# Fused attention and expert layers on one core: a product for four batches at once by way of device memory, and a fixed order from step 36

## The chip, the cores and the metric

The kernel runs on one core of one Trainium2 chip. The metric is the device time of one execution in microseconds, less is better. The engines are named as in the profile: PE (TensorE matmul) with its weight loads PEld, DVE (VectorE), ACT (ScalarE), POOL (GpSimd) and SP (SyncE, which issues the DMAs here).

## What is computed

```python
# q, k, v: 8 batches x 8 heads x 576 x 64;  phi: 8 x 8 x 576 x 32;  w1: 4 x 512 x 1024;  w2: 4 x 1024 x 512
a = softmax(phi, axis=2)                       # over the sequence
k_m = einsum('bhsm,bhsd->bhmd', a, k)          # 32 memory rows per head
v_m = einsum('bhsm,bhsd->bhmd', a, v)
attn = softmax(q @ k_m.T / 8)
x = (attn @ v_m), heads side by side           # 4608 x 512
p = domain_probs / domain_probs.sum(-1)
out = sum over 4 experts e of p[:, e] * (relu(x @ w1[e]) @ w2[e])
```

All values are float32.

## The kernel before

The kernel never forms x. For each batch and expert it multiplies v_m with w1 (the product `vw`, 256 rows of 8 heads × 32 memory rows, by 1024), and then attn with `vw`. Every operand of a large matmul is split into a rounded part (ACT's copy to float32r) and a rest (DVE's subtraction); a product of two such operands is three matmuls: high × high, high × low, low × high. So nearly every tile costs one piece on ACT and one on DVE, named below by its output: `w` (w1 and w2 splits, L118 and L119), `vw` (L379, L380), `kvs` and `tl` (k and v, L218, L219, L204, L205), `a` (softmax of phi, transposed, L187, L188), `AT` (attn transposed).

Batches go in four pairs (k = 0 to 3). A pair passes through 4 experts, each of 32 steps, which makes 128 steps for a pair and 512 in all (`PAIR`, `LAST`). A step s does:

- `first(s + 2)` (L405): six matmuls of attn and `vw` into a PSUM tile `p1`, 256 or 320 wide, then relu. ACT makes the high part of `h` (L427), DVE the rest (L429). At width 320 there is a second piece of 64, `hm`.
- `second(s)` (L434): h with w2, three matmuls of 512 for each of two tiles, or of three tiles where `hm` is complete, into `p2`. After 8 steps DVE adds the finished tiles into `acc` (L460, L462), and the last expert's go out.
- side work from a table `plan[s]`: the attention of the next two batches, and the splits and `vw` products of the next expert.

Side work of a batch: `phi_max`, `phi_exp`, `phi_norm`, `phi_turn` (softmax of phi, transposed); `kv_split`, `kv_mm` (k_m and v_m of four head pairs into PSUM tiles `x`); `kv_out` copies x to SBUF (`xs`, ACT L241), `kv_fold` transposes it (PE L249, into `kvp`), `kv_pick` takes the parts out (`kvT`); `write_vt` splits v_m into `vt`; then scores, softmax and `transposes`. `vw_mm` (L361) makes one product of v_m and w1 for a pair of batches, three matmuls (L364 to L366) into a tile `pv`, and `vw_out` (L369) takes it out in two halves of 64 rows, one for each batch.

The side tiles and `p1` share four PSUM buffers (tag `pm`). Loads go through a ring of `STAGE` tiles, all by SP, each issued some loads ahead (`stage_ahead`, L90). The prologue stands in `tc.manual_schedule()`, where each engine has its instructions in program order; from step 0 on a scheduler orders them.

Of the kernel before, what the change touches and what calls it, by code (L numbers as in the profile page):

```python
# [32 lines left out]
PSUM = bass.MemoryType.PSUM  # L34

# [13 lines left out]
STAGE = 5  # L49
KVS = 2  # L50
AHEAD = 2

# [3 lines left out]
VW_AT = 26  # L56

UNITS_EVEN = (0, 4, 6, 6, 7, 9, 10, 13, 16, 19, 22, 37, 42, 42, 46, 49, 49)
UNITS_EVEN_0 = (29, 33, 36, 37, 37, 39, 40, 43, 46, 49, 50, 64, 69, 73, 73, 80, 81)
UNITS_ODD = (63, 66, 68, 69, 69, 71, 72, 75, 78, 81, 84, 99, 104, 104, 109, 111, 112)  # L60
# [9 lines left out]
def body(ctx: ExitStack, tc: tile.TileContext, qm, qt, kv, kvt, phi, prob, w1, w2, out):  # L70
    nc = tc.nc
    pool = lambda name, **k: ctx.enter_context(tc.tile_pool(name=name, bufs=1, **k))
    const, wp, work, att = pool("const"), pool("wp"), pool("work"), pool("att")
    psum = pool("psum", space=PSUM)

    ident = const.tile([P, P], F32, name="ident")
    make_identity(nc, ident)
    kvT = [const.tile([P, 2, NP, 2 * M], F32, name=f"kvT{i}") for i in range(2)]
    for t in kvT:
        nc.gpsimd.memset(t, 0.0)  # L80
# [3 lines left out]
    def source(key):  # L84
        kind, *i = key
        return {"kv": kv, "kvt": kvt, "qm": qm, "qt": qt, "w1": w1, "w2": w2}[kind][tuple(i)]
# [45 lines left out]
    def unit_w2(k, e, j2, eng=nc.vector):  # L132
        def emit(raw):
            for i in range(2):
                t = wp.tile([P, 2, DM], F32R, name="w2", tag="w2", bufs=NJ + 2)
                split(t, raw[:, i, :], eng)
                w2t[k, e, 2 * j2 + i] = t
        return ("w2", e, j2), emit

# [36 lines left out]
    def phi_turn(b, g):  # L176
        if g == 0:
            st["a", b] = att.tile([P, NP, NC, 2, 2 * M], F32R, name="a", tag="a")
        ph, a = st["ph", b], st["a", b]
        tp = psum.tile([P, 4, 2, 2 * M], F32, name="tpa", tag="pm", bufs=4)  # L180
        for c in range(4):
            nc.tensor.transpose(
                tp[:, c].rearrange("p a m -> p (a m)"), ph[:, g, c * P:(c + 1) * P], ident
            )
        src = tp.rearrange("p c a m -> p a c m")
        dst = a[:, 2 * g:2 * g + 2, :4]
        nc.scalar.copy(dst[:, :, :, 0, :], src)  # L187
        nc.vector.tensor_sub(dst[:, :, :, 1, :], src, dst[:, :, :, 0, :].bitcast(F32))  # L188

    def phi_turn_tail(b):  # L190
        ph, a = st["ph", b], st["a", b]
        tp = psum.tile([P, NP, 2 * M], F32, name="tpb", tag="pm", bufs=4)
        for g in range(2):
            nc.tensor.transpose(
                tp[:, 2 * g:2 * g + 2].rearrange("p a m -> p (a m)"), ph[:, g, 512:], ident
            )
        nc.scalar.copy(a[:, :, 4, 0, :], tp)
# [24 lines left out]
    def kv_mm(b, hp, c2):  # L222
        if hp % 2 == 0 and c2 == 0:
            st["x", b, hp // 2] = psum.tile([P, 2, 2 * P], F32, name="x", tag="pm", bufs=4)
        x, a, t = st["x", b, hp // 2], st["a", b], st["kvs", b, hp, c2]
        for i in range(2):
            c = 2 * c2 + i
            lhs = a[:, hp, c].rearrange("p s m -> p (s m)")
            for s in range(2):
                nc.tensor.matmul(x[:, hp % 2, :], lhs, t[:, s, i, :], start=c + s == 0, stop=False)  # L230

    def kv_mm_tail(b, hp):
        nc.tensor.matmul(
            st["x", b, hp // 2][:, hp % 2, :],
# [4 lines left out]
    def kv_out(b, hp):  # L239
        xs = att.tile([P, 2 * P], F32, name="xs", tag="xs", bufs=2)  # L240
        nc.scalar.copy(xs, st["x", b, hp // 2][:, hp % 2, :])  # L241
# [11 lines left out]
    def kv_pick(b, g):  # L253
        kvd = kvT[b % 2][:, :, 2 * g:2 * g + 2]
        kvp = st["kvp", b, g].rearrange("p h w c -> p w h c")
        for i in range(2):
            r, m = slice(64 * i, 64 * i + 64), slice(M * i, M * i + M)
            if i == 0:
                nc.scalar.copy(kvd[r, :, :, m], kvp[r, :, :, m])
            else:  # L260
                nc.vector.tensor_copy(kvd[r, :, :, m], kvp[r, :, :, m])
        for i in range(2):
            r, m = slice(64 * i, 64 * i + 64), slice(M * i, M * i + M)
            lo = slice(2 * M + M * i, 2 * M + M * i + M)
            nc.vector.tensor_add(kvd[r, :, :, m], kvd[r, :, :, m], kvp[r, :, :, lo])
# [15 lines left out]
    def write_vt(b, a=slice(0, 2)):  # L281
        k, odd = b // 2, b % 2
        if ("vt", k) not in st:
            st["vt", k] = att.tile([P, NP, 2, P], F32R, name="vt", tag="vt", bufs=2)
        vt = st["vt", k].rearrange("p (a two) h c -> p a two h c", two=2)
        v = kvT[odd].rearrange("p w (a two) c -> p w a two c", two=2)
        for par in range(2):
            dst = vt[:, a, par ^ odd, :, 64 * par:64 * par + 64]
            src = v[:, 1, a, par, :]
            nc.scalar.copy(dst[:, :, 0, :], src)  # L290
            nc.vector.tensor_sub(dst[:, :, 1, :], src, dst[:, :, 0, :].bitcast(F32))
# [4 lines left out]
    def scores_mm(b, t0, q, hps=range(NP)):  # L296
        nt, n = tiles(t0)
        kvd = kvT[b % 2]
# [3 lines left out]
        for hp in hps:  # L302
            for i in range(nt):
                nc.tensor.matmul(  # L304
                    sc[:n, i, hp, :], q[:, hp, i * P:i * P + n], kvd[:, 0, hp, :],
# [3 lines left out]
    def scores_exp(b, t0):  # L309
# [7 lines left out]
        nc.vector.tensor_sub(av, scv, mx[:n, :nt * H].broadcast_to([n, nt * H, M]))  # L317
        nc.scalar.activation(av, av, AF.Exp, scale=float(D) ** -0.5)
        st["at", b, t0] = at
# [14 lines left out]
    def unit_scores(b, t0):  # L334
        def emit(q):
            scores_mm(b, t0, q)
            scores_exp(b, t0)
            soft(b, t0)
        return q_key(b, t0), emit

    def transposes(b, t0):
# [3 lines left out]
        at, at_t = st["at", b, t0], st["AT", b]  # L345
        tp = psum.tile([P, 2, 256], F32, name="tp", tag="pm", bufs=4)
        for i in range(nt):
            for g in range(2):
# [4 lines left out]
                )  # L353
        c = slice(t0 * P, t0 * P + nt * n)
# [6 lines left out]
    def vw_mm(k, fh, hp, tag):  # L361
        vt, w = st["vt", k], w1t[fh, hp]
# [6 lines left out]
    def vw_out(ps, fh, hp, odds):  # L369
        g = hp // 2  # L370
        for odd in odds:
            if hp % 2 == 0:
                vw[odd, fh, g] = att.tile(
                    [P, 2, 512], F32R, name="vw", tag=f"vw{odd}", bufs=4 + odd
                )
            q = (hp % 2) ^ odd
            r = slice(64 * q, 64 * q + 64)
            t = vw[odd, fh, g]
# [3 lines left out]
    def vw_out_by_copy(ps, fh, hp):  # L382
        g, r = hp // 2, slice(64 * (hp % 2), 64 * (hp % 2) + 64)
        if hp % 2 == 0:
            vw[0, fh, g] = att.tile([P, 2, 512], F32R, name="vw", tag="vw0", bufs=4)
        t = vw[0, fh, g]
# [5 lines left out]
    def vw_unit(k, e, fh, hp, odds, tag):  # L392
        vw_out(vw_mm(k, fh, hp, tag), fh, hp, odds)


    hs, mid, acc, po = {}, {}, {}, {}
# [8 lines left out]
    def first(s):  # L405
# [7 lines left out]
        for g in range(2):  # L413
            w = vw[odd, j // 4, g]
# [19 lines left out]
    def second(s):  # L434
# [13 lines left out]
        if j < NJ - 1:  # L448
            return
        if e == 0:  # L450
# [5 lines left out]
        for t, _ in left:  # L456
# [15 lines left out]
    def att_units(b):  # L472
        u = [lambda g=g: phi_turn(b, g) for g in range(2)] + [lambda: phi_turn_tail(b), unit_tail(b)]
        u += [unit_kv(b, hp) for hp in range(NP)]
        u += [lambda: write_vt(b)]
        u += [unit_scores(b, t0) for t0 in (0, 2, 4)]
        u += [lambda t0=t0: transposes(b, t0) for t0 in (0, 2, 4)]
# [5 lines left out]
    rest = [unit_scores(0, t0) for t0 in (2, 4)] + [lambda t0=t0: transposes(0, t0) for t0 in (2, 4)]  # L483
# [3 lines left out]
    for s, u in zip(REST_0, rest):  # L487
        at(s, u)

# [3 lines left out]
    for fh in range(2):  # L493
        for g in range(2):
            at(W1_1[2 * fh + g], unit_w1(0, 0, fh, g))
            for i in range(2):
                vw_at(VW_1[4 * fh + 2 * g + i], 0, 0, fh, 2 * g + i, (1,))
    for k in range(NG):
        for e in range(E):
            s = k * PAIR + e * STEPS  # L500
            nk, ne = (k, e + 1) if e + 1 < E else (k + 1, 0)
            if nk < NG:
                for j2 in range(4):
                    at(s + W2_AT[j2], unit_w2(nk, ne, j2))
                n = 0
                for fh in range(2):
                    for g in range(2):
                        at(s + W1_AT[2 * fh + g], unit_w1(nk, ne, fh, g))
                        for i in range(2):
                            vw_at(s + VW_AT + n, nk, ne, fh, 2 * g + i, (0, 1))  # L510
                            n += 1
        if k + 1 < NG:
            b = 2 * k + 2
            for bb, U in ((b, UNITS_EVEN_0 if k == 0 else UNITS_EVEN), (b + 1, UNITS_ODD)):
                s0 = k * PAIR
                at(s0 + U[0], lambda bb=bb: load_phi(bb))
# [34 lines left out]
    with tc.manual_schedule():  # L551
        raw = {key: take(later) for later, key in enumerate(early)}
        stage_ahead(len(early) + 4)
        nc.sync.dma_start(pt, prob)
        keep_warm(10)
        dve, gps = nc.vector, nc.gpsimd
        write_vt(1)
# [26 lines left out]
        for hp in (2, 3):  # L584
# [3 lines left out]
            if hp == 2:  # L588
                for i in range(2):
                    kv_fold(0, i)  # L590
        kv_pick(0, 0)
        write_vt(0, slice(0, 1))
        w1g = [raw["w1", 0, 0, g] for g in range(2)]
        for hp in (2, 3):
            kv_out(0, hp)
        split_w1(w1g[0], 0, 0, gps)
        q = raw["qm", 0, 0]
        scores_mm(0, 0, q, (0, 1))
        for hp in (2, 3):
            kv_fold(0, hp)  # L600
        kv_pick(0, 1)
        scores_mm(0, 0, q, (2, 3))
        split_w1(w1g[0], 0, 1, dve)
        write_vt(0, slice(1, 2))
        split_w1(w1g[1], 0, 2, gps)
        split_w1(w1g[1], 0, 3, gps)
        for i in range(2):
            t = wp.tile([P, 2, DM], F32R, name="w2", tag="w2", bufs=NJ + 2)
            nc.scalar.copy(t[:, 0, :], raw["w2", 0, 0][:, i, :])
            w2t[0, 0, i] = t  # L610
        scores_exp(0, 0)
        for i in range(2):
            t = w2t[0, 0, i]
            dve.tensor_sub(t[:, 1, :], raw["w2", 0, 0][:, i, :], t[:, 0, :].bitcast(F32))
# [5 lines left out]
        vw_out(pv[1], 0, 1, (0,))  # L620
        transposes(0, 0)
        keep_warm(4)
        vw_out(pv[3], 0, 3, (0,))
# [4 lines left out]
    for s in range(LAST):  # L628
        run_plan(s)
        first(s + AHEAD)  # L630
        second(s)
# [36 lines left out]
```

## Time and profile before

| | us |
|---|---|
| median of 3 runs (lowest, highest) | 1428.31 (1426.05, 1429.47) |
| the profiled execution | 1428.84 |
| its span, first to last instruction | 1427.1 |
| mean granted clock of PE | 0.996 of full |
| PE busy / DVE busy / ACT busy | 1412.3 / 837.2 / 620.2 |
| DMA | 115.20 MB, mean 81 GB/s |

In the rows of the profile, a group has its line, engine, operation, output<-input, shape, count, then busy time and mean ns of one, then the engine's idle time ahead of it and what ended that. A row of windows has start:end, length, then for PE, PEld, DVE, ACT and POOL the busy time and the number of instructions, then PE's granted clock, the share of DMA and GB/s. A row of the timeline has start, length, engine, line, and in brackets a wait ahead of it and its releaser; a row of the chain has start, length, engine, tile and line; a row of waits has the total, the number of times and the longest. A DMA row has KB each and the median us from issue to landing.

### The profile page before, as it was taken

What the parts mean: (1) busy time and instruction counts of PE and PEld (TensorE: products, weight loads), DVE (VectorE), ACT (ScalarE), POOL (GpSimd) and SP (SyncE); (2) the same over time, 40 slices, a digit from 0 to 9 for tenths busy, and PEclk for the clock granted to TensorE, in tenths of its full rate; (3) what the DMA queues carried; (4) which work ended last, traced back from release to release, by engine and by line L of the source; (5) the groups of instructions that cost most, each with busy time, mean ns of one, the idle gap of its engine ahead of it and who ended that gap; (6) DMA issues with size and microseconds to landing.
All of it is one profiled execution on the core that took longest, in us unless ns stands there. A gap on an engine that the chain in (4) does not pass through costs nothing.

```text
span 1427.1 us, 20830 instructions
## 1 busy us (share of the span) xinstructions
PE 1412.3 (99%) x7808; PEld 1233.5 (86%) x7808; DVE 837.2 (59%) x1853; ACT 620.2 (43%) x1543; POOL 27.8 (2%) x27
## 2 busy tenths in 40 slices
PE   7999999999999999999999999999999999999998
PEld 6888888888888888888888888888888888888887
DVE  7876638666385654837547375573846446272722
ACT  6655426453263533635335362452625234161521
POOL 3300000000000000000000000000000000000000
PEclk8999999999999999999999999999999999999999
DMA  6632303323141120412214121140323103030001
GB/s 245 198 118 75 121 28 126 104 64 104 39 161 61 64 89 16 137 58 78 94 63 135 59 88 65 46 130 18 107 75 96 60 25 94 1 119 1 1 30 38
DMA packets 35957, 115.20 MB, mean 81 GB/s; under 512 B 3984, under 2 KB 5136, under 8 KB 35856
## 3 DMA queue, kind: packets, MB, share of 16 engines
q1 hardware_dynamic: 35856, 113.86, 24.5%
q8 instruction: 62, 1.02, 0.3%
q14 instruction: 39, 0.32, 0.1%
HBM read 104.41 MB, written 9.44 MB: 80 GB/s over the span
## 4 chain that ended last, share of the span: by engine, by line
PE 92%; DMA 2%; DVE 2%; ACT 2%; issue 1%; POOL 0%; SPq 0%; ACTq 0%
PE p L446 18%; PE p L447 18%; PE p L445 18%; PE p L415 9%; PE p L417 9%; PE p L416 9%; PE sc L304 2%; PE pv L366 2%; PE pv L364 2%; PE x L230 2%; PE pv L365 2%; DMA stage<-in_w 1%; PE tp L349 1%; PE kvp L249 1%; ACT w L118 0%
## 5 line engine op out<-in xcount | busy, mean ns | idle before, releaser
L446 PE MATMUL p<-w,h 128*128 128x512 f32 x1024 | 404.3, 395 | 0.0
L447 PE MATMUL p<-w,h 128*128 128x512 f32 x1024 | 402.8, 394 | 0.0
L445 PE MATMUL p<-w,h 128*128 128x512 f32 x1024 | 402.7, 393 | 0.0
L427 ACT ACTIVATE h<-p 128x256 fp32r<-128x256 f32 x512 | 195.2, 382 | 331.5 <-PE p L417 294.3
L429 DVE SCALAR_TENSOR_TENSOR h<-p,h 128x256 fp32r<-128x256 f32 x512 | 213.9, 418 | 206.3 <-ACT h L427 110.0
L415 PE MATMUL p<-AT,vw 128*128 128x256 f32 (+1 forms) x1024 | 308.2, 301 | 0.0
L417 PE MATMUL p<-AT,vw 128*128 128x256 f32 (+1 forms) x1024 | 304.3, 297 | 0.1
L416 PE MATMUL p<-AT,vw 128*128 128x256 f32 (+1 forms) x1024 | 303.6, 297 | 0.0
L447 PEld LDWEIGHTS p<-w,h 128*128 128x128 f32 x1024 | 192.4, 188 | 43.3 <-DVE nm L154 0.2
L119 DVE TENSOR_TENSOR w<-stage,w 128x512 fp32r<-128x512 f32 x259 | 175.9, 687 | 78.4 <-ACT w L118 77.1
L445 PEld LDWEIGHTS p<-w,h 128*128 128x128 f32 x1024 | 193.2, 189 | 23.3
L446 PEld LDWEIGHTS p<-w,h 128*128 128x128 f32 x1024 | 192.6, 188 | 22.0
L416 PEld LDWEIGHTS p<-AT,vw 128*128 128x128 f32 x1024 | 194.5, 190 | 19.5 <-DVE AT L356 0.3
L415 PEld LDWEIGHTS p<-AT,vw 128*128 128x128 f32 x1024 | 194.0, 189 | 19.1
L417 PEld LDWEIGHTS p<-AT,vw 128*128 128x128 f32 x1024 | 193.5, 189 | 0.7 <-DVE vw L380 0.6
L118 ACT CAST w<-stage 128x512 fp32r<-128x512 f32 x262 | 159.6, 620 | 79.1 <-DMA stage<-in_w 47.3
L380 DVE TENSOR_TENSOR vw<-pv,vw 64x512 fp32r<-64x512 f32 x254 | 172.1, 685 | 8.9 <-ACT vw L379 5.5
L429 DVE SCALAR_TENSOR_TENSOR hm<-p,hm 128x64 fp32r<-128x64 f32 x256 | 56.0, 219 | 201.9 <-ACT h L427 200.9
L379 ACT CAST vw<-pv 64x512 fp32r<-64x512 f32 x254 | 145.5, 580 | 58.5 <-DVE vw L380 42.6
L427 ACT ACTIVATE hm<-p 128x64 fp32r<-128x64 f32 x256 | 56.6, 221 | 227.9 <-PE p L417 227.9
L462 DVE SCALAR_TENSOR_TENSOR acc<-p,pt,acc 128x512 f32<-128x512 f32 x96 | 67.8, 741 | 2.6 <-PE p L447 2.6
L366 PE MATMUL pv<-w,vt 128*128 128x512 f32 x136 | 53.7, 395 | 0.0
(81 smaller groups left out, 1020.5 us busy)
## 6 DMA issues: line engine op xcount, KB each, us to landing
stage<-in_w SPq DMA_DIRECT2D x132, 512.0 KB, 3.8
stage<-in_kv SPq DMA_DIRECT2D x32, 512.0 KB, 4.1
stage<-in_qm SPq DMA_DIRECT2D x16, 512.0 KB, 3.7
out<-acc SPq DMA_DIRECT2D x32, 256.0 KB, 2.1
ph<-in_phi SPq DMA_DIRECT2D x16, 288.0 KB, 3.5
stage<-in_kvt SPq DMA_DIRECT2D x8, 512.0 KB, 3.8
stage<-in_qt SPq DMA_DIRECT2D x8, 128.0 KB, 3.2
out<-accm SPq DMA_DIRECT2D x4, 256.0 KB, 2.2
```

What stands on the lines that cost most here:

```text
L118: nc.scalar.copy(dst[:, 0, :], raw)
L119: eng.tensor_sub(dst[:, 1, :], raw, dst[:, 0, :].bitcast(F32))
L379: nc.scalar.copy(t[r, 0, :], ps[r])
L380: nc.vector.tensor_sub(t[r, 1, :], ps[r], t[r, 0, :].bitcast(F32))
L415: nc.tensor.matmul(ps, w[:, 0, f], at_t[:, g, 0, c], start=g == 0, stop=False)
L416: nc.tensor.matmul(ps, w[:, 0, f], at_t[:, g, 1, c], start=False, stop=False)
L417: nc.tensor.matmul(ps, w[:, 1, f], at_t[:, g, 0, c], start=False, stop=g == 1)
L427: nc.scalar.activation(t[:, 0, to], ps[:, at_], AF.Relu)
L429: nc.vector.scalar_tensor_tensor(t[:, 1, to], ps[:, at_], 0.0, t[:, 0, to].bitcast(F32), ALU.max, ALU.subtract)
L445: nc.tensor.matmul(po[t], x[:, 0, :], w[:, 0, :], start=j == 0, stop=False)
L446: nc.tensor.matmul(po[t], x[:, 0, :], w[:, 1, :], start=False, stop=False)
L447: nc.tensor.matmul(po[t], x[:, 1, :], w[:, 0, :], start=False, stop=j == NJ - 1)
```

## The change

- **Four batches at once.** For expert 3 of pairs 0 and 1 and all experts of pairs 2 and 3, `four` multiplies v_m of four batches with w1: one head's 32 memory rows of four batches are the 128 rows of the result. High and low part of v_m lie one below the other in the 128 contracted rows (`vs`, made by `write_vs`), and the 64 rows of w1 stand twice (`w1d`), so a product is two matmuls (L506). ACT and DVE take it out in 128 rows into `vst` (L508, L509; the ring `kvs`, now 3 buffers), a DMA writes it to device memory (`to_memory`, L492), and `load_vw` (L531) reads for each batch the 32 rows of four heads into a `vw` tile. The other pairs and experts keep `vw_mm` with three matmuls.
- **Order.** Steps 36 to 511 stand in `tc.manual_schedule()`. The side work is cut into parts, each a step or more behind the one that makes its input; `accumulate` stands a step behind its `second`.
- **Tiles.** `kT` has four buffers, v_m its own tile `v` and a rounded copy `vh`; `vt` is kept for both pairs 0 and 1; heads are reordered by `TURN`; one `x` tile for each head pair; `STAGE` 4 in place of 5; 9 w2 buffers in place of 10.
- **Prologue.** Ten more `keep_warm` matmuls, the w2 subtractions behind `soft` and the `vw` evictions, `kv_pick` and `write_vt` in more and smaller pieces.

```diff
-STAGE = 5
-KVS = 2
+STAGE = 4
+KVS = 3
+FREE = 36
+VW_LOAD_AT = ((20, 25), (28, 32))
+FOUR = (3, 0)
+FOUR_AT = ((6, 8, 10, 12), (14, 16, 18, 20))
+FOUR_LAG = 2
...
+    def to_memory():
+        for key, t in done:
+            vwd[key] = dram.tile([P, 2, 512], F32, name="vwd" + "".join(map(str, key)))
+            nc.sync.dma_start(vwd[key], t.bitcast(F32))
+        done.clear()
...
+    def four(n, e, fh, h, w):
+
+        to_memory()
+        g, vs = h // 4, st["vs", n]
+        ps = psum.tile([P, 512], F32, name="pv", tag="pm", bufs=4)
+        for a in range(2):
+            nc.tensor.matmul(ps, vs[:, g, h % 4, :], w[:, a, :], start=a == 0, stop=a == 1)
+        t = att.tile([P, 2, 512], F32R, name="vst", tag="kvs", bufs=KVS)
+        nc.scalar.copy(t[:, 0, :], ps)
+        nc.vector.tensor_sub(t[:, 1, :], ps, t[:, 0, :].bitcast(F32))
+        done.append(((n, e, fh, g, h % 4), t))
...
+    def load_vw(k, e, odd, fh):
+        b = 2 * k + odd
+        for g in range(2):
+            t = vw_tile(k, e, odd, fh, g)
+            for h in range(4):
+                r = slice(M * slot(b, h), M * slot(b, h) + M)
+                nc.sync.dma_start(t[r].bitcast(F32), vwd[b // 4, e, fh, g, h][r])
...
+    def attention(b, s, scores, turns):
...
+            at(s + 12 + 3 * hp, multiply)
+            at(s + 13 + 3 * hp, lambda hp=hp: kv_out(b, hp))
+        for g in range(2):
+            at(s + 18 + 6 * g, lambda g=g: [kv_fold(b, 2 * g + i) for i in range(2)])
+            at(s + 19 + 6 * g, lambda g=g: kv_pick(b, g))
...
-    for s in range(LAST):
-        run_plan(s)
-        first(s + AHEAD)
-        second(s)
+    def steps(a, b):
+        for s in range(a, b):
+            run_plan(s)
+            accumulate()
+            first(s + AHEAD)
+            second(s)
+
+    steps(0, FREE)
+    with tc.manual_schedule():
+        steps(FREE, LAST)
+        accumulate()
```

Three places in the order of instructions. In these rows `p_…` numbers are those of the `p1` and `p2` tiles, `w_…` those of splits.

On DVE, where batch 5's phi and k, v stand among w and vw pieces. Before (here in steps near 197):

```order
L429 SCALAR_TENSOR_TENSOR h<-p_5829,h 128x256
L205 TENSOR_TENSOR tl<-stage,tl 64x512
L380 TENSOR_TENSOR vw<-pv,vw 64x512 x2
L429 SCALAR_TENSOR_TENSOR h<-p_5856,h 128x256
L462 SCALAR_TENSOR_TENSOR acc<-p_5655,pt,acc 128x512
L380 TENSOR_TENSOR vw<-pv,vw 64x512
L462 SCALAR_TENSOR_TENSOR acc<-p_5659,pt,acc 128x512
L380 TENSOR_TENSOR vw<-pv,vw 64x512
L429 SCALAR_TENSOR_TENSOR h<-p_5884,h 128x256
```

After (the h of steps 160 to 162, so steps 158 to 160 of the plan):

```order
L567 SCALAR_TENSOR_TENSOR h<-p_5310,h 128x256
L143 TENSOR_TENSOR w_5328<-stage,w_5328 128x512
L474 TENSOR_TENSOR vw<-pv,vw 64x512 x2
L232 TENSOR_TENSOR a<-tpa,a 128x2x4x64
L253 TENSOR_TENSOR tl<-stage,tl 64x512 x2
L567 SCALAR_TENSOR_TENSOR h<-p_5353,h 128x256
L143 TENSOR_TENSOR w_5369<-stage,w_5369 128x512
L474 TENSOR_TENSOR vw<-pv,vw 64x512 x2
L246 TENSOR_TENSOR a<-tpb,a 128x4x64
L267 TENSOR_TENSOR kvs<-stage,kvs 128x512 x2
L603 TENSOR_SCALAR acc<-p_5116,pt 128x512
L603 TENSOR_SCALAR acc<-p_5120,pt 128x512
```

The next row is the h of step 162. Between two h stood 3 or 4 pieces, and now 6 and 8.

On ACT, at the copies xs that `kv_fold` reads (batch 3's third and fourth head pair). Before, with the fold's result in the next row (`kvT<-kvp`):

```order
L427 ACTIVATE h<-p_2732 128x256
L427 ACTIVATE hm<-p_2732 128x64
L218 CAST kvs<-stage 128x512 x2
L241 COPY xs<-x 128x256 x2
L259 COPY kvT_76<-kvp 64x2x2x32
L427 ACTIVATE h<-p_2781 128x256
```

After, from the second copy of a group to the pick (batch 3's first two head pairs):

```order
L289 COPY xs<-x 128x256
L266 CAST kvs<-stage 128x512 x2
L565 ACTIVATE h<-p_2428 128x256
L473 CAST vw<-pv 64x512 x2
L142 CAST w_2456<-stage 128x512
L565 ACTIVATE h<-p_2459 128x256
L473 CAST vw<-pv 64x512 x2
L142 CAST w_2483<-stage 128x512
L565 ACTIVATE h<-p_2501 128x256
```

Both copies stood together directly ahead of the pick. Now the second one stands three h ahead of it.

On ACT, at the products of v_m and w1 (late experts). Before:

```order
L118 CAST w_8189<-stage 128x512
L379 CAST vw<-pv 64x512
L118 CAST w_8344<-stage 128x512
L427 ACTIVATE h<-p_8284 128x256
L379 CAST vw<-pv 64x512
L118 CAST w_8244<-stage 128x512
```

After, at `four`:

```order
L508 CAST vst<-pv 128x512
L142 CAST w_7598<-stage 128x512
L565 ACTIVATE h<-p_7601 128x256
L565 ACTIVATE hm<-p_7601 128x64
L508 CAST vst<-pv 128x512
L142 CAST w_7628<-stage 128x512
```

The copies of 64 rows have become one of 128 rows in each step, directly ahead of a w split and the relu, and it writes a buffer that a DMA has read.

More of the change, by code (lines that the diff above doesn't have):

```diff
@@ L69, in body @@
 @with_exitstack
[L70 removed]
+def body(ctx: ExitStack, tc: tile.TileContext, qm, qt, kv, kvt, phi, prob, w1, w1d, w2, out):
     nc = tc.nc
@@ L253, in kv_pick @@
     def kv_pick(b, g):
[L254 to L265, printed above, removed]
+        if g == 0:
+            st["v", b] = att.tile([P, NP, M], F32, name="v", tag="v", bufs=2)
+        for w in range(2):
+            for i in range(2):
+                r, m = slice(64 * i, 64 * i + 64), slice(M * i, M * i + M)
+                lo = slice(2 * M + M * i, 2 * M + M * i + M)
+                a = slice(2 * g, 2 * g + 2)
+                dst = st["v", b][r, a] if w else kT[b % 4][r, a, m]
+                src = st["kvp", b, g][r, :, w]
+                (nc.vector.tensor_copy if i else nc.scalar.copy)(dst, src[:, :, m])
+                nc.vector.tensor_add(dst, dst, src[:, :, lo])
     def unit_kv(b, hp):
@@ L447, in second, with accumulate @@
             nc.tensor.matmul(po[t], x[:, 1, :], w[:, 0, :], start=False, stop=j == NJ - 1)
-        if j < NJ - 1:
+        if j == NJ - 1:
+            ended.append((k, e, t0, [t for t, _ in left]))
+    def accumulate():
+        if not ended:
             return
+        k, e, t0, left = ended.pop()
         if e == 0:
@@ L472, in att_units, with write @@
     def att_units(b):
-        u = [lambda g=g: phi_turn(b, g) for g in range(2)] + [lambda: phi_turn_tail(b), unit_tail(b)]
+        u = [lambda g=g: (phi_turn(b, g), phi_turn_out(b, g)) for g in range(2)]
+        u += [lambda: (phi_turn_tail(b), phi_turn_tail_out(b)), unit_tail(b)]
         u += [unit_kv(b, hp) for hp in range(NP)]
-        u += [lambda: write_vt(b)]
+        def write():
+            v_hi(b)
+            if b < 4:
+                write_vt(b)
+            write_vs(b)
+        u += [write]
         u += [unit_scores(b, t0) for t0 in (0, 2, 4)]
-        u += [lambda t0=t0: transposes(b, t0) for t0 in (0, 2, 4)]
+        u += [lambda t0=t0: (transposes(b, t0), transposes_out(b, t0)) for t0 in (0, 2, 4)]
         return u
```

295 lines of the change are left out of this document (219 added, 76 removed).

## The prediction

> **What bounds the kernel now.** I read the page's busy shares and its chain first, then windows of the span, then the times at which single matmuls start.
>
> ```profile
> span 1427.1 us, 20830 instructions
> PE 1412.3 (99%) x7808; PEld 1233.5 (86%) x7808; DVE 837.2 (59%) x1853; ACT 620.2 (43%) x1543; POOL 27.8 (2%) x27
> ```
>
> ```profile
> 0.00:20.00 20.00, 14.70 (x81) 13.76 (x82) 12.76 (x28) 12.29 (x28) 7.53 (x12) 0.83 0.93 336
> 20.00:40.00 20.00, 16.60 (x98) 13.98 (x97) 18.00 (x35) 15.25 (x33) 6.59 (x5) 0.91 0.41 143
> ...
> 1000.00:1100.00 100.00, 100.00 (x556) 87.22 (x555) 62.05 (x132) 45.91 (x109) 0.00 (x0) 1.00 0.27 89
> ```
>
> PE is busy 99% of the span; in the last window, like most, it never pauses, at clock 1.00. Its idle time lies mainly in the first 40 us (5.3 + 3.4). A record's end is modelled, so I take the distance between starts as the cost:
>
> ```profile
> 1001.01 0.39 PE L364 MATMUL pv<-w,vt 128*128 128x512 f32 x1
> ...
> 1001.70 0.28 PE L415 MATMUL p<-AT,vw 128*128 128x256 f32 x1
> ...
> 1002.41 0.39 PE L445 MATMUL p<-w,h 128*128 128x512 f32 x1
> ...
> 1003.80 0.39 PE L364 MATMUL pv<-w,vt 128*128 128x512 f32 x1
> ```
>
> The three matmuls of one product of v_m and w1 take 1001.01 to 1001.70: 0.69 us, 0.230 each, not the record's 0.39. `first` (six of width 256) takes 0.71 and `second` (six of 512) 1.39, so a plain step takes 2.10 us.
>
> **Term 1, matmuls that go.** Before there are 136 products of three matmuls, 408. After there are 56 of these (168) and 80 products for four batches of two matmuls (160), 328. So 80 fewer × 0.230 = 18.4 us, on an engine without slack. The order shows them gone, so that the change removes nothing is not a rival.
>
> ```profile
> L366 PE MATMUL pv<-w,vt 128*128 128x512 f32 x136 | 53.7, 395 | 0.0
> L379 ACT CAST vw<-pv 64x512 fp32r<-64x512 f32 x254 | 145.5, 580 | 58.5 <-DVE vw L380 42.6 <-PE pv L366 10.3
> L380 DVE TENSOR_TENSOR vw<-pv,vw 64x512 fp32r<-64x512 f32 x254 | 172.1, 685 | 8.9 <-ACT vw L379 5.5
> L119 DVE TENSOR_TENSOR w<-stage,w 128x512 fp32r<-128x512 f32 x259 | 175.9, 687 | 78.4 <-ACT w L118 77.1
> ```
>
> ACT and DVE lose 80 evictions each as well (160 of 64 rows become 80 of 128 rows): 80 × 0.580 and 80 × 0.685 us. Neither engine bounds the whole, so the sum has nothing for it; it loosens steps that had slack.
>
> **Term 2, a wait of PE that goes.** Before, ACT makes the copies xs directly ahead of the fold that reads them:
>
> ```profile
> 440.53 0.40 PE L446 MATMUL p<-w,h 128*128 128x512 f32 x1
> 441.78 0.71 PE L249 MATMUL kvp<-ident,xs 128*128 128x128 f32 x4 [0.85 <-ACT xs L241]
> ```
>
> ```profile
> PE kvp L249 <- ACT xs L241: 1.9, 3, 0.9
> ```
>
> From start to start 1.25 us where 0.23 is due: 1.02 lost, 0.17 more than the 0.85 recorded. Three such waits lose 1.9 + 3 × 0.17 = 2.4 us. Afterwards the copy stands two steps ahead of the fold: minus 2.4.
>
> **Term 3, the fixed order on DVE.** The relu parts of h for step s+2 stand behind all side work that the program puts into step s. The densest place is batch 5's chain among the w1 and w2 splits, steps 155 to 160. DVE's prices:
>
> ```profile
> L429 DVE SCALAR_TENSOR_TENSOR h<-p,h 128x256 fp32r<-128x256 f32 x512 | 213.9, 418 | 206.3 <-ACT h L427 110.0 <-ACT hm L427 93.9
> L429 DVE SCALAR_TENSOR_TENSOR hm<-p,hm 128x64 fp32r<-128x64 f32 x256 | 56.0, 219 | 201.9 <-ACT h L427 200.9
> L219 DVE TENSOR_TENSOR kvs<-stage,kvs 128x512 fp32r<-128x512 f32 x54 | 37.2, 722 | 8.7 <-ACT kvs L218 8.4
> L460 DVE TENSOR_SCALAR acc<-p,pt 128x512 f32<-128x512 f32 x32 | 22.5, 741 | 0.0
> L188 DVE TENSOR_TENSOR a<-tpa,a 128x512 fp32r<-128x512 f32 x16 | 10.7, 684 | 3.9 <-ACT a L187 3.9
> L167 DVE TENSOR_SCALAR ph<-ph,zs 128x576 f32<-128x576 f32 x16 | 8.7, 541 | 0.5
> L205 DVE TENSOR_TENSOR tl<-stage,tl 64x512 fp32r<-64x512 f32 x12 | 8.3, 689 | 0.4
> L198 DVE TENSOR_TENSOR a<-tpb,a 128x256 fp32r<-128x256 f32 x8 | 3.3, 417 | 0.5 <-ACT a L197 0.5
> L168 DVE COPY ph<-ph 128x64 f32<-128x64 f32 x16 | 3.0, 190 | 0.3
> L166 DVE RECIPROCAL zs<-zs 128x1 f32<-128x1 f32 x16 | 2.5, 159 | 0.3
> L165 DVE TENSOR_SCALAR zs<-zs 128x1 f32<-128x1 f32 x16 | 2.4, 149 | 2.8 <-ACT ph L160 2.3
> L291 DVE TENSOR_TENSOR vt<-kvT,vt 128x64 fp32r<-128x64 f32 x4 | 0.7, 223 | 0.3 <-ACT vt L290 0.3
> ```
>
> By the order, steps 155 to 160 hold 12 vw subtractions (8.22 us), 6 w splits (4.12), 6 h (2.51), two `phi_norm` of 1.04 (2.08), a (1.79), tl ×2 (1.38), kvs ×2 (1.44), acc ×2 (1.48), and 6 small pieces of `write_vs`, which the trace lacks, at the nearest row's 0.223 (1.34): 24.4 us up to h of step 162. PE comes to that h after seven plain steps (14.7), five products (3.45), two and a half groups of four phi transposes, nine x matmuls and one `first` (0.71):
>
> ```profile
> 175.47 0.94 PE x L230 x8
> ...
> 238.52 0.44 PE tpa L182 x4
> ```
>
> 14.7 + 3.45 + 1.1 + 1.06 + 0.71 = 21.0 us. DVE is 3.4 us late. Likewise steps 47 to 49: 3 w splits, 20 small pieces, two `phi_norm`, 2 acc and 3 h with hm are 12.0 us. PE comes after 9.8 us (a `first` of width 320 is 0.89 in proportion, a `second` of three tiles 2.07, four transposes 0.44: steps of 2.28, 2.96 and 3.40, then product and transposes 1.13) to the `first` of step 50, which takes over the PSUM buffer that the last of these h reads: 2.2 late. Five more places (near steps 61, 147, 169, 178 and 190) put picks, kvs or scores among splits. I give them 2.4 together; each may be 0 to 2.2.
>
> ```profile
> 570.00:590.00 20.00, 20.00 (x112) 17.33 (x111) 19.05 (x35) 15.21 (x32) 0.00 (x0) 1.00 0.42 132
> ```
>
> This row of before is the lower bound: DVE at 95% costs PE nothing there, with an h after every four long pieces. Now up to eight stand between two h. Term 3: plus 8.0, bounds 0 and 3.4 + 2.2 + 5 × 2.2 = 16.6.
>
> **Term 4, by way of memory.** SP gets 80 writes of 512 KB and 320 reads of 128 KB more. ACT's copy into `vst` waits until the write from the same buffer, three products ago, has landed; the relu is queued behind that copy.
>
> ```profile
> stage<-in_w SPq DMA_DIRECT2D x132, 512.0 KB, 3.8
> ...
> out<-acc SPq DMA_DIRECT2D x32, 256.0 KB, 2.1
> ...
> pt<-in_prob SPq DMA_DIRECT2D x1, 72.0 KB, 7.3
> ```
>
> ```profile
> 0.74 0.39 SPq L146
> ...
> 24.15 2.19 DVE w L614 x2
> 26.34 0.61 DVE z L326
> ```
>
> A step with such a product takes PE at least 2.10 + 0.46 = 2.56 us, three steps 7.7. A buffer needs copy and subtraction (0.58 + 0.69), an issue (0.39) and the landing. At 3.8 that is 5.5: hidden, with 2.2 to spare. At 7.3, the worst row (in the first 20 us, DMA 93% busy), it is 9.0: not hidden. The rows of 512 KB are nearest: I take 3.8, the term is 0. The reads are issued nine steps or more (over 19 us) before use; `load_vw` reads and stage loads share SP's queue with the writes, and 19 us hold that too.
>
> [...]
>
> **Term 5, the start.** The two w2 subtractions (2.19 us, L614 above) move behind `soft`. But `kv_pick` and `write_vt` become about twice as many instructions: some 10 small ones at 0.223 on the same path, 2.2 us, and ten more warm-up matmuls. Bounds minus 2.2 and plus 2.2; I take 0.
>
> **Sum.** 1428.84 (the profiled execution: its span and 1.74 around it) − 18.4 − 2.4 + 8.0 = 1416.0. It stands 0.5 above the median of the runs shown, 1428.31: 1415.5.
>
> **Rivals.**
> - The fixed order costs nothing, as in 570:590: 1428.3 − 20.8 = 1407.5. For it: all side inputs are made a step ahead, and 80 evictions are gone. Against: the 3.4 and 2.2 above.
> - The fixed order costs all it can, and the clock falls. The bound of 16.6 gives 1424.1. The clock has a row:
>
> ```profile
> 29.30 0.66 PE L349 MATMUL tp<-ident,at 128*128 128x128 f32 x4 [1.98 <-DVE at L329]
> ...
> 32.07 0.41 PE L415 MATMUL p<-AT,vw 128*128 128x256 f32 x1
> 32.28 0.42 PE L416 MATMUL p<-AT,vw 128*128 128x256 f32 x1
> ```
>
> After that wait of 1.98 us, matmuls of width 256 start 0.21 apart instead of 0.12, for eight of them: 0.7 us lost. Seven such waits would add 5: 1429. [...]
> - Slower: the write lands late. If it takes more than 6.0 us, each product costs PE (1.66 + landing) / 3 − 2.56. From 6.5 us on this takes the forecast gain (80 × 0.16 = 12.8); at 7.3 it is 80 × 0.43 = 34: 1449. For it: one write and half a stage load per step are 0.79 MB in 2.56 us, 307 GB/s, where 336 was the most seen, at 93%. Against: wide steps are longer, and the median landing is 3.8.
>
> **How the numbers follow.** The forecast (1410 to 1420) has 0.50, no cost of the order 0.18, the full cost with or without the clock 0.16 (half of it below 1424), late writes 0.08; 0.08 is left for the start and for what I don't see. A range of 1406 to 1424 leaves out the late writes, half of the full cost and a few at its low end, 0.2. This kernel's measurement tells 0.2% (2.9 us) from no change: faster is below 1425.4. Forecast, no cost, 0.10 of the full cost and 0.06 of the rest give 0.84; within 0.2% 0.05; slower 0.11.
>
> **What would show it.** The new profile should have 160 matmuls from `four`, PE busy for some 18 us less, no wait of kvp for xs, and DVE named as the releaser of PE in steps 155 to 162. Waits of `vst` copies for DMA, or a landing above 6 us, would prove term 4 wrong; no DVE waits, term 3. What would make it wrong altogether is a wait in each of the 80 products.

## The result, and the profile after

The changed kernel takes 1436.55 us (median of 4 runs, 1435.92 to 1438.51), the kernel before 1427.78 in the same series (4 runs, 1426.05 to 1429.47). The ratio is 1.0064, 95% interval 1.0046 to 1.0081: slower by 0.64%, where I forecast 0.9% faster. The profiled execution has this span and PE share:

```profile
span 1434.6 us, 21439 instructions
PE 1399.7 (98%) x7748; PEld 1217.1 (85%) x7748; DVE 815.8 (57%) x1877; ACT 562.7 (39%) x1496; POOL 29.1 (2%) x31
```

PE is busy 12.6 us less and the span is 7.5 us longer, so PE's idle time rose from 14.8 to 34.9 us. The waits of PE name the new releasers (us in total, times, longest):

```profile
PE p L583 <- DVE acc L605: 6.6, 5, 3.1
PE p L553 <- DVE vw L474: 5.2, 5, 1.7
PE tpa L223 <- DVE ph L208: 3.0, 2, 1.8
PE p L553 <- ACT xs L289: 2.6, 2, 1.3
```

None of them has to do with device memory. ACT's copies into `vst` wait for PE, all 80, and never for a write; then the landings, from the page's list of DMA issues (the slowest of the 80 writes took 6.5 us):

```profile
ACT vst L508 <- PE pv L506: 125.0, 80, 2.6
```

```profile
vwd<-vst SPq DMA_DIRECT2D x80, 512.0 KB, 3.3
vw<-vwd SPq DMA_DIRECT2D x320, 128.0 KB, 4.0
```

To place the loss I took, for every matmul, the distance to the next start less the median distance of its line and shape, and summed this excess by stretches of steps (us). It is what PE waits, and what it loses to a lower clock; the medians are rounded to 0.01 us, so a sum over hundreds of matmuls can be off by several us, and some are negative.

| kernel | prologue | steps 0 to 35 | 36 to 127 | 128 to 255 | from 256 |
|---|---|---|---|---|---|
| before | 9.8 | 2.8 | 1.7 | 2.4 | 0.9 |
| after | 8.4 | 11.1 | 8.4 | 14.3 | -1.8 |
| x1_planned | 10.4 | 10.9 | 0.6 | 0.5 | -2.9 |
| y1_v_parts_late | 10.3 | 9.1 | 0.5 | -0.8 | -2.8 |
| y2_order_mended | 9.9 | 7.7 | 1.6 | 8.6 | -4.4 |
| y3_two_buffers | 9.9 | 6.3 | 0.8 | -0.7 | 8.8 |

From step 36 on the excess rose by 15.9 us and in steps 0 to 35 by 8.3. The largest single wait is PE's at step 48, in the third tile of a `second`:

```profile
190.62 0.39 PE L585 MATMUL p<-w,h 128*128 128x512 f32 x1
194.08 0.50 PE L583 MATMUL p<-w,hm 128*128 128x512 f32 x1 [3.07 <-DVE acc L605]
194.41 0.50 PE L584 MATMUL p<-w,hm 128*128 128x512 f32 x1
```

What DVE did meanwhile:

```profile
190.18 0.68 DVE L143 TENSOR_TENSOR w<-stage,w 128x512 fp32r<-128x512 f32 x1
190.88 0.19 DVE L354 CAST vt<-vh 64x64 fp32r<-64x64 f32 x1
...
192.00 0.21 DVE L355 TENSOR_TENSOR vt<-v,vh 64x64 fp32r<-64x64 f32 x1
...
192.61 0.52 DVE L208 TENSOR_SCALAR ph<-ph,zs 128x576 f32<-128x576 f32 x1
193.17 0.20 DVE L209 COPY ph<-ph 128x64 f32<-128x64 f32 x1
193.28 1.41 DVE L605 SCALAR_TENSOR_TENSOR acc<-p,pt,acc 128x512 f32<-128x512 f32 x2
```

There are four buffers `p2`. At step 16 of an expert three tiles begin while the two finished at step 15 are not yet added up, so the third tile needs `accumulate` first; and that stands behind all side work of the step. Seven experts show it at their step 16: 3.2 us of excess at step 48, 2.4 at 176, and 0.4 to 0.6 at 80, 144, 272, 304 and 336. (The expectations below count these steps one higher.) The windows show what follows the two long waits (PE's clock is the last figure but two):

```profile
190.00:194.10 4.10, 1.03 (x6) 0.53 (x4) 3.93 (x16) 0.97 (x4) 0.00 (x0) 1.00 0.00 1
194.10:198.00 3.90, 3.90 (x14) 3.47 (x15) 2.91 (x10) 0.17 (x2) 0.00 (x0) 0.56 0.31 86
198.00:202.00 4.00, 4.00 (x23) 3.50 (x22) 1.17 (x3) 0.81 (x3) 0.00 (x0) 1.00 0.12 47
...
569.80:573.50 3.70, 3.68 (x13) 3.28 (x14) 3.57 (x12) 0.20 (x2) 0.00 (x0) 0.54 0.27 74
```

After 3.07 and 2.22 us of waiting the clock is 0.56 and 0.54 for some 3.8 us: 3.9 × 0.44 + 3.7 × 0.46 = 3.4 us lost besides the waits. The length of a wait does not decide this alone. In x4_order_alone (below) PE waits as long at the same step, and the clock stays at 1.00:

```profile
194.66 0.50 PE L583 MATMUL p<-w,hm 128*128 128x512 f32 x1 [3.07 <-DVE acc L605]
```

```profile
194.70:198.60 3.90, 3.90 (x21) 3.39 (x22) 2.72 (x7) 0.98 (x3) 0.00 (x0) 1.00 0.31 91
```

In the traces of the two kernels all changes of the clock lie whole multiples of 3.41 us apart: in the changed kernel it falls at 10.24, 194.56, 570.02 and 1433.60 and rises at 13.65, 197.97 and 573.44, and the two falls behind these waits, at 194.56 and 570.02, are 110 times 3.41 us apart. In the 3.41 us ahead of these two PE was idle, by its records, for 2.93 and 2.22 us, and in the kernel before for 1.98 us ahead of the fall at 30.24; behind 1.61 us, in the 3.41 us from 505.17 and from 614.40 on, the clock stayed at 1.00. Why it also did behind the 3.07 us in x4_order_alone is not shown.

PE is "busy" in the stretches at half clock (3.41 us of the 3.41 from 194.56 on), which is one reason why busy time fell by less than 18.

The second place is the products at steps 154 to 159. One product's two copies on ACT, and the two subtractions on DVE:

```profile
500.29 0.58 ACT L473 CAST vw<-pv 64x512 fp32r<-64x512 f32 x1
504.08 0.58 ACT L473 CAST vw<-pv 64x512 fp32r<-64x512 f32 x1 [3.20 <-DVE vw L474]
```

```profile
503.35 0.69 DVE L474 TENSOR_TENSOR vw<-pv,vw 64x512 fp32r<-64x512 f32 x1
504.69 0.68 DVE L474 TENSOR_TENSOR vw<-pv,vw 64x512 fp32r<-64x512 f32 x1 [0.64 <-ACT vw L473]
```

The second copy reads the PSUM tile that DVE is still to read, and in this kernel it waits for DVE: 3.20 us, with ACT's relu queued behind it. Then DVE waits 0.64 us for the copy, with its own h queued behind.

### The profile page after: what moved, and what is told of

Its sections match the earlier page's. It is cut to its first block, busy times and chain, and to the rows that moved or that the text cites. A ratio compares the mean times of both kernels' runs of the same rounds, so it can differ in the third digit from the quotient of the medians.

```text
span 1434.6 us, 21439 instructions
## 1 busy us (share of the span) xinstructions
PE 1399.7 (98%) x7748; PEld 1217.1 (85%) x7748; DVE 815.8 (57%) x1877; ACT 562.7 (39%) x1496; POOL 29.1 (2%) x31
## 4 chain that ended last, share of the span: by engine, by line
PE 88%; DVE 6%; ACT 3%; DMA 2%; issue 1%; ACTq 0%; DVEq 0%
PE p L585 17%; PE p L583 17%; PE p L584 17%; PE p L553 9%; PE p L555 9%; PE p L554 9%; PE pv L506 2%; PE sc L383 2%; PE x L278 2%; DVE vw L474 1%; DVE w L143 1%; ACT vw L473 1%; DMA vwd<-vst 1%; PE tp L433 1%; ACT w L142 1%
## 5 line engine op out<-in xcount | busy, mean ns | idle before, releaser
L143 DVE TENSOR_TENSOR w<-stage,w 128x512 fp32r<-128x512 f32 x259 | 179.0, 693 | 11.2 <-ACT w L142 4.9
L509 DVE TENSOR_TENSOR vst<-pv,vst 128x512 fp32r<-128x512 f32 x80 | 55.3, 691 | 95.5 <-ACT vst L508 95.5
L508 ACT CAST vst<-pv 128x512 fp32r<-128x512 f32 x80 | 47.0, 587 | 125.0 <-PE pv L506 125.0
L474 DVE TENSOR_TENSOR vw<-pv,vw 64x512 fp32r<-64x512 f32 x94 | 64.4, 687 | 25.6 <-ACT vw L473 24.5
L473 ACT CAST vw<-pv 64x512 fp32r<-64x512 f32 x94 | 54.3, 581 | 43.7 <-DVE vw L474 34.1
```

Source lines behind the costliest of these rows:

```text
L143: eng.tensor_sub(dst[:, 1, :], raw, dst[:, 0, :].bitcast(F32))
L473: nc.scalar.copy(t[r, 0, :], ps[r])
L474: nc.vector.tensor_sub(t[r, 1, :], ps[r], t[r, 0, :].bitcast(F32))
```

## The experiments

**Each half of the change alone.** First the planner's order with the 4-batch products kept, then the fixed order without them.

```diff
-FREE = 36
+FREE = LAST
```

> The changed kernel with the fixed order taken away: steps 36 to 511 are ordered by the planner as in the kernel before, and the 4-batch products, their writes and their loads stay. Theory A (the loss is the fixed order: PE's excess over its nominal pitches is 40.3 us against 17.6 before, and about 18 us of the difference lies in steps 36 to 337): most of those 18 us go, some 1418 us, and 1415 to 1422. Theory B (the loss is the way by memory, whose 400 more transfers run beside the products): the time stays within 4 us of 1436.5. Theory C (the loss is in the prologue and steps 0 to 35, which the planner already orders): 1430 us or more, since only what comes after step 36 changes.

Measured: 1412.1 us (4 runs, 1411.16 to 1413.0), ratio 0.9894 (0.9878 to 0.9911).

```profile
PE 1391.9 (99%) x7748; PEld 1216.1 (86%) x7748; DVE 809.7 (57%) x1877; ACT 578.1 (41%) x1496; POOL 29.5 (2%) x31
```

```profile
PE x L278 <- DVE a L232: 2.7, 1, 2.7
...
PE p L585 <- DVE nm L195: 1.0, 1, 1.0
PE p L553 <- DVE hm L567: 0.9, 2, 0.5
```

The same 7748 matmuls, with no wait for `acc` and none over 0.5 us after step 36. The time falls below the expected 1415: the fixed order costs 24.4 us, all that the change loses and more. Theory B falls, and theory C as the main loss; its smaller loss in steps 0 to 35 is still there (10.9 us of excess against 2.8).

```diff
-FOUR = (3, 0)
+FOUR = (4, 4)
-        vt = vts[b // 2].rearrange(...)
+        vt = vts[b // 2 % 2].rearrange(...)
...
-        at(s + 26, lambda: (v_hi(b), write()))
-        at(s + 27, lambda: write_vs(b))
+        at(s + 26 if b < 6 else 2 * PAIR + 40 + b, lambda: (v_hi(b), write_vt(b)))
```

> The changed kernel with the fixed order but without the 4-batch products: all products are computed pair by pair (408 matmuls of 512 again), nothing goes by way of memory, and the arrays v_m for the 4-batch products are no longer made for batches 2 to 7. Theory A (order): 80 matmuls of 0.230 us come back, +18.4 us, and DVE gets in steps 224 to 479 the copies of products that it had in steps 128 to 191, where it held PE for about 16 us in two experts; so 1455 us at least, up to 1480. Theory B (memory): about 1428 plus the small cost of the order, 1425 to 1440.

Measured: 1463.82 us (1462.07 to 1465.04), ratio 1.0258 (1.0243 to 1.0273). PE's waits:

```profile
PE p L553 <- DVE vw L474: 10.9, 9, 2.1
PE p L583 <- DVE acc L605: 6.3, 2, 3.2
```

27.3 us more than with the 4-batch products, 18.4 of it by the price of the 80 matmuls (PE's busy time rose by 19.2). So the 4-batch products save their matmuls under the fixed order too; the waits for `vw` doubled, as theory A says. No run has the 4-batch products without the new tiles and the new prologue.

**Two pieces of the order.**

```diff
         for s in range(a, b):
+            if s >= FREE:
+                accumulate()
             run_plan(s)
-            accumulate()
+            if s < FREE:
+                accumulate()
```

> The changed kernel with the accumulation of a finished group of row tiles (L599 to L605) ahead of the step's side work in each engine's order, from step 36, instead of behind it. Theory A in its first part (PE waits for DVE because the accumulation stands behind side work: 3.2 us at step 49, 2.4 at step 177, and 0.4 to 0.6 us in five steps with 4-batch products, with the slower clock after the two long ones 1 to 2 us more each): 8 to 11 us faster, 1425.5 to 1428.5. If DVE is simply too full at those steps, the same side work is late for the next matmul that needs it, and the gain is under 3 us (over 1433.5).

Measured: 1430.12 us (9 runs, 1428.51 to 1432.03), ratio 1.0024 (1.0014 to 1.0035): 6.4 us faster, between the two expectations. PE's waits:

```profile
PE p L553 <- DVE h L567: 2.6, 2, 1.3
...
PE p L583 <- DVE acc L605: 1.6, 1, 1.6
```

The short waits at the five steps are gone and so is the one at step 48, but DVE's h comes 1.35 us late at step 50 instead, and 1.6 us remain at 176. Behind neither does the clock fall (from 568.2 to 576 it is 1.00). It falls elsewhere instead, at 503.8, and stays at half for 6.8 us; the excess of steps 155 to 160 is as large as before.

```diff
         for odd in odds:
             ...
             nc.scalar.copy(t[r, 0, :], ps[r])
+        for odd in odds:
+            ...
             nc.vector.tensor_sub(t[r, 1, :], ps[r], t[r, 0, :].bitcast(F32))
```

> The changed kernel with the two ACT copies of one product (L473, batches 2k and 2k+1) side by side ahead of the two DVE subtractions (L474), instead of copy, subtraction, copy, subtraction. In the trace the second copy waits for the first subtraction and the second subtraction 0.65 us for that copy, in 0.58 + 0.69 + 0.58 + 0.69 us. Theory A in its second part (these waits on DVE, behind which everything else of a fixed order queues, hold PE at steps 157 to 159 for 7.5 us, at 61 to 63 for 2.7 and at 190 and 191 for 3.9): 5 to 10 us faster, 1426.5 to 1431.5. If DVE is too full there whatever the order of the four: within 3 us of 1436.5.

Measured: 1431.35 us (6 runs, 1429.33 to 1432.15), ratio 1.0028 (1.0016 to 1.004): 5.2 us faster, at the low end. The two copies, and the two subtractions, now run through (timelines of ACT and of DVE):

```profile
502.21 1.17 ACT L473 CAST vw<-pv 64x512 fp32r<-64x512 f32 x2
```

```profile
502.64 1.39 DVE L477 TENSOR_TENSOR vw<-pv,vw 64x512 fp32r<-64x512 f32 x2
```

The excess of steps 188 to 192 falls from 3.8 to 1.5 us, of 155 to 160 only from 7.5 to 5.7; the rest there goes only when batch 5's work moves away, in the next kernel.

**The fixed order mended.** Both edits above, and:

```diff
-    5: (PAIR + 22, (...
+    5: (PAIR + 28, (...
...
-        at(s + 26, lambda: (v_hi(b), write()))
-        at(s + 27, lambda: write_vs(b))
+        late = 8 if b == 2 else 0
+        at(s + 26 + late, lambda: (v_hi(b), write()))
+        at(s + 27 + late, lambda: write_vs(b))
...
-    at(4, lambda: (v_hi(0), write_vs(0)))
+    at(19, lambda: (v_hi(0), write_vs(0)))
```

> The changed kernel with its fixed order mended at the places where PE waited: the accumulation ahead of the side work (x2_sum_first, -6.4 us), the two ACT copies of a product side by side (x3_casts_together, -5.2 us), batch 5's attention work six steps later (156 instead of 150, away from the products of steps 154 to 159), batch 2's v_m arrays eight steps later (56, 57 instead of 48, 49), and batch 0's at step 19 instead of 4. Theory A (a fixed order costs what its crowded steps cost, no more): the gains add up and the shifts take 4 to 7 us more, 1416 to 1421, still above x1_planned. Rival (any fixed order holds PE about as much, the waits only move): 1424 us or more.

Measured: 1416.66 us (1416.32 to 1417.79), ratio 0.9929 (0.9914 to 0.9943). Theory A holds: steps 155 to 160, 7.5 us of excess, have none left. y1_v_parts_late, below, also has batch 0's `write_vs` at step 19, under the planner's order: against it the mended order still costs 7.0 us. Some 4.5 of this is one wait at step 176, and the clock behind it:

```profile
PE p L586 <- DVE acc L608: 2.8, 1, 2.8
```

```profile
553.40:557.40 4.00, 4.00 (x21) 3.88 (x20) 3.41 (x11) 0.00 (x0) 0.00 (x0) 0.60 0.30 102
```

**How near the way by memory is to costing something.** x1_planned with:

```diff
-STAGE = 4
-KVS = 3
+STAGE = 5
+KVS = 2
```

> The kernel of x1_planned with two buffers instead of three in the ring that the 4-batch products share with the attention's kv parts (KVS 2), and five stage buffers instead of four. It asks how near the way by memory is to costing something. My threshold for the landing of a 512 KB write was 6.5 us with three buffers, one step of about 2.8 us less with two, so 3.7 us; the writes land in a median of 3.3 us. So: most products just pass, within 4 us of x1_planned (1412.1). If the landing is what bounds, each of the 80 products waits up to 1 us and more: 1425 us or more.

Measured: 1420.83 us (1420.66 to 1421.58), ratio 0.9957 (0.9943 to 0.9972): 8.7 us slower than x1_planned, between the expectations.

```profile
ACT vst L508 <- DMA vwd<-vst: 4.4, 6, 2.0
...
PE p L553 <- DVE vst L509: 3.6, 2, 1.8
```

Six of 80 copies now wait for a write, though the median lands in 3.0 us. PE loses nothing by five of these waits, the longest (1.95 us, at 713.6) among them, and 0.19 us by the sixth. PE's two long waits stand elsewhere, at 804.7 and 982.5, where ACT waits for PE with a `w` split, and the copies of two products stand together behind that split:

```profile
802.74 0.62 ACT L142 CAST w<-stage 128x512 fp32r<-128x512 f32 x1 [1.86 <-PE pv L506]
803.26 1.07 ACT L508 CAST vst<-pv 128x512 fp32r<-128x512 f32 x2
```

In x1_planned these copies come one by one. So the excess from step 256 on, 8.8 us against -2.9, comes from another order of the planner's and from the clock, which falls behind both waits (its mean is 0.996 in each of the four runs, and 0.997 to 1.000 in x1_planned's), and not from PE waiting for writes. That the planner chose this order because of the smaller ring is likely and not shown, since five stage buffers came with it.

**The first 36 steps.** x1_planned with batch 0's `write_vs` at step 19 (the last edit of the mended order):

> The kernel of x1_planned (steps 36 on ordered by the planner, 1412.1 us) with one piece of early side work moved: the eight small DVE instructions and four ACT copies that write batch 0's part of the operand of the 4-batch products (L369, L370, write_vs) go from step 4 to step 19. Theory C, narrowed (the 5 to 6 us more of PE waits in steps 2 to 10 come from side work that the change adds there: in the trace of x1_planned PE waits 1.20 and 1.95 us at step 5 for DVE, which does these instructions just then, one of them taking 1.19 us): 2 to 3.5 us faster than x1_planned, ratio to the kernel before 0.987 to 0.988. If the waits of step 5 belong to the softmax chain of batch 1 alone: within 1 us of x1_planned, 0.989 to 0.990.

Measured: 1409.65 us (1409.09 to 1411.08), ratio 0.988 (0.9865 to 0.9894), 2.45 us below x1_planned; the intervals of the two overlap, but in the trace the second wait that the expectation names, 1.79 us as recorded, is gone, and one of 0.44 us for a `w` piece is left. The rest of the early excess (9.1 against 2.8 us; the next expectation has an earlier count of it) lies mostly in steps 0 to 12, in five waits of PE where the kernel before has none. The two longest:

```profile
PE p L585 <- DVE nm L195: 1.3, 1, 1.3
PE kvp L297 <- ACT xs L289: 1.2, 1, 1.2
```

I sought the cause in three places. The first was the stage ring, in y1_v_parts_late and in the kernel before:

```diff
-STAGE = 4
+STAGE = 5
-W2_AT = (20, 23, 25, 27)
+W2_AT = (27, 29, 31, 33)
...
-        t = wp.tile([P, 2, DM], F32R, name="w2", tag="w2", bufs=NJ + 1)
+        t = wp.tile([P, 2, DM], F32R, name="w2", tag="w2", bufs=NJ)
```

> The kernel of y1_v_parts_late with five stage buffers again as in the kernel before (STAGE 5), three buffers kept in the ring of the 4-batch products, and the room taken from the ring of w2 (8 tiles instead of 9, and in the first expert of all w2 is prepared in steps 27 to 34 instead of 20 to 28). Theory C, second part (the rest of the early loss is the fifth stage buffer: PE's excess over nominal in steps 0 to 35 is 3.0 us in the kernel before, 8.6 in y1_v_parts_late, 5.7 in y3_two_buffers, which has five): 2 to 4 us faster than y1_v_parts_late (1409.65), ratio to the kernel before 0.985 to 0.987. If the fifth buffer does nothing there, or the shorter ring of w2 takes back what it gives: 0.988 or more.

Measured: 1413.08 us (1411.6 to 1413.49), ratio 0.99 (0.9886 to 0.9913): 3.4 us slower than y1_v_parts_late. Early excess 7.6 instead of 9.1, of which 1.7 is a fall of the clock at 52.5 us that y1_v_parts_late does not have; but 2.2 instead of -2.8 from step 256 on, where the shorter ring of w2 may have its part.

```diff
-STAGE = 5
+STAGE = 4
```

> The kernel before with one part of the change alone: four stage buffers instead of five. Theory C, second part: 2 to 4 us slower than the kernel before in steps 0 to 35, and since its stage loads wait for DVE to free a buffer all along, perhaps some more later: ratio 1.0015 to 1.004. If the fifth stage buffer does nothing: within 0.1%.

Measured: 1428.3 us (11 runs, 1426.68 to 1430.87), ratio 1.0008 (0.9999 to 1.0017): no difference that can be told in the time. The traces, one execution of each, have one: some 2 us more excess in steps 0 to 35 than the kernel before, in two waits at steps 4 and 10 that it doesn't have:

```profile
PE p L447 <- DVE nm L154: 1.0, 1, 1.0
PE x L230 <- POOL kvs L219: 0.9, 1, 0.9
```

A wait for `nm` at step 4 stands in y1_v_parts_late too. So the fourth stage buffer less is some 2 us of the early excess, as theory C says at its low end, and not the larger part. Then two parts of the prologue, each in y1_v_parts_late:

```diff
         scores_exp(0, 0)
+        for i in range(2):
+            t = w2t[0, 0, i]
+            dve.tensor_sub(t[:, 1, :], raw["w2", 0, 0][:, i, :], t[:, 0, :].bitcast(F32))
         pv = [vw_mm(0, 0, hp, ("p2", 4)) for hp in range(4)]
...
-        for i in range(2):
-            t = w2t[0, 0, i]
-            dve.tensor_sub(t[:, 1, :], raw["w2", 0, 0][:, i, :], t[:, 0, :].bitcast(F32))
```

> The kernel of y1_v_parts_late with the two w2 subtractions of the prologue back ahead of the first products and of soft, where the kernel before has them. My term 5 priced this move at 0. Theory C, third part (the move gains some 2 us up to step 0 and gives them back, with interest, in steps 0 to 8, where DVE now has this work in competition with batch 1's softmax; PE's excess in steps 0 to 35 is 9.1 us against 2.8 in the kernel before): step 0 starts 1 to 2 us later, steps 0 to 8 lose 2 to 4 us less, and the time falls by 0.5 to 2 us below y1_v_parts_late (1409.65), ratio to the kernel before 0.986 to 0.9875. If the move is a plain gain of DVE work hidden later: 1 to 2 us slower, 0.989.

Measured: 1409.26 us (1409.07 to 1412.01), ratio 0.9881 (0.9866 to 0.9895): no difference. The trace has both halves, step 0 starting 1.6 us later and steps 0 to 8 losing 3.1 us less; 1.1 us of that is lost again by step 12.

```diff
-        keep_warm(3)
...
-        keep_warm(5)
...
-        keep_warm(2)
```

> The kernel of y1_v_parts_late without the ten additional warm-up matmuls of the prologue (of 3, 5 and 2). In the profile of the kernel before the clock of PE is 0.87 in the first 40 us, with them 0.96. If they buy that clock: step 0 starts 1 to 3 us later without them and the time rises by as much, ratio 0.989 to 0.990. If they only fill a wait (their matmuls of 0.15 us stand where PE idles): within 1 us, 0.987 to 0.9885.

Measured: 1409.73 us (1408.73 to 1412.13), ratio 0.9883 (0.9866 to 0.9899): no difference. The last kernel was meant to be the best, with the copies side by side in y1_v_parts_late:

> The kernel of y1_v_parts_late with the two ACT copies of one product side by side (x3_casts_together). With the planner's order the waits between ACT and DVE in these copies hold up little (PE's excess from step 36 on is 0.8 us in x1_planned): within 1.5 us of y1_v_parts_late, some 1409 us, ratio to the kernel before 0.986 to 0.989.

Measured: 1411.13 us (1410.45 to 1413.15), ratio 0.9887 (0.987 to 0.9903): not told apart from y1_v_parts_late. What cures the fixed order does nothing for the planner's.

## Why the prediction was wrong

- **Term 1** (-18.4) holds. In x1_planned 18.4 saved, 6.8 less excess from step 36 on (the table's last three columns) and 8.7 more before it make -16.5; the span fell by 16.0. The 6.8 are not waits: PE's recorded waits after step 36 are 1.9 us before and 1.6 in x1_planned. Most of it is a plain step of width 256, 2.119 us at its median before and 2.094 in every kernel with the change; why, stays open.
- **Term 2** (-2.4) came true as a row and not as a gain: after step 36 PE never waits with `kvp` for xs, but `first` waits twice for xs, 2.6 us, since ACT's copy also frees the PSUM buffer that `first` takes over. In x1_planned both kinds are gone after step 36, and one wait of `kvp` for xs, 1.4 us, stands at step 10.
- **Term 3** (+8.0, bounds 0 to 16.6) is the step that failed: 24.4 us, above its upper bound. The places were mostly right, the sizes not. Steps 155 to 160 have 7.5 us of excess, not 3.4: I added up DVE's instructions, and left out its waits for ACT in the copies of products (x3_casts_together). Steps 47 to 52 have 5.3, not 2.2: I counted `acc` among DVE's load, and let the `first` of step 50 wait, where the third `p2` tile of step 48 waits for `accumulate` itself, two steps earlier. Near 61, 176 and 190 there are 2.9, 4.0 and 3.8, together 10.7, where I gave five places 2.4; at 147 and 169 there is nothing. The five short waits for `accumulate` (3.1 us, by the excess of their whole steps) were not in the sum at all. These places make 26.6 us; all of steps 36 to 511 has 20.9, and -1.8 in x1_planned, both with the shorter plain steps.
- **The clock**, which I put in a rival with seven waits of 0.7 us, fell twice behind waits in the steps, of 3.07 and 2.22 us, and cost 1.7 us each time. Behind a wait of 1.73 us, at step 158, the clock stayed at 1.00, and in x4_order_alone behind one of 3.07 us. So two of these three waits of over 2 us cost 1.7 us besides themselves, and one did not.
- **Term 4** (0) holds, with landings of 3.3 us where I took 3.8. Late writes were no danger with three buffers: the slowest took 6.5 us, above my 6.0, and held nothing; in y4_best and z1_five_stages one copy each waited, 0.7 and 1.2 us. With two, 6 of 80 copies waited, though by the median they should all have passed, and PE lost next to nothing by it.
- **Term 5** (0, bounds ±2.2) failed by its bounds: steps 0 to 35 lost 8.3 us more, the prologue 1.4 less. Batch 0's `write_vs`, a piece at step 4 that I had left out, is about 2 of it: with the prologue, x1_planned has 8.7 us more excess than before, y1_v_parts_late 6.8. The stage ring, which the sum did not have, is some 2 us more, by b1_before_four_stages. Moving the w2 subtractions was worth 0, as priced, and taking the warm-up matmuls out changed nothing. What takes the rest, some 5 us, stays open.
- **The rivals.** "The order costs nothing" gave 1407.5, and x1_planned and y1_v_parts_late come to 1412.1 and 1409.65 where it is true. That they come so near is partly luck: the early loss of 8.7 and 6.8 us and the shorter plain steps, neither of them forecast, nearly cancel. The one for the full cost of the order was the right mechanism and still 7.5 us too low.

## What to carry to other kernels

When a scheduler's order is replaced by the program's, don't only add up an engine's instructions over a crowded stretch: find for each of its pieces who waits for it and what stands ahead of it, and count each handover between two engines inside a piece as a wait with a queue behind it. Work that frees a buffer belongs ahead of work that only prepares. A rewrite that brings a saving and a new order is to be run with each alone: here all but the fixed order was worth -14.7 us, and the fixed order +24.4.

## What the runs showed of the hardware

Beside POOL two small DVE instructions took longer than elsewhere (0.67 and 1.19 us), and each ended 0.05 us behind one of POOL's. POOL in the changed kernel, then DVE:

```profile
46.88 2.75 POOL L253 TENSOR_TENSOR tl<-stage,tl 64x512 fp32r<-64x512 f32 x2 [17.92 <-ACT tl L252]
49.70 4.22 POOL L267 TENSOR_TENSOR kvs<-stage,kvs 128x512 fp32r<-128x512 f32 x3
```

```profile
49.01 0.67 DVE L209 COPY ph<-ph 128x64 f32<-128x64 f32 x1
...
50.26 0.75 DVE L410 TENSOR_SCALAR z<-z 128x16 f32<-128x16 f32 x1
...
52.78 1.19 DVE L369 CAST vs<-vh 64x64 fp32r<-64x64 f32 x1
```

The copy L209 takes 0.20 us elsewhere (193.17 above) and 0.67 here, ending as POOL's first row ends (49.68 and 49.63); L369 takes 0.19 at its median and 1.19 here, ending with POOL's last (53.97 and 53.92). L369 is one of the eight `write_vs` instructions at step 4; the 1.0 us that it lost is probably part of the 2.45 us that moving them gained, which no run shows apart.
